# Order of transfers in the first chunk of a fused attention and gated-MLP kernel: weight sets, queries and keys, packed outputs

## The chip, the core and the metric

The kernel runs on one core of a Trainium2 chip. The metric is the device time of one execution in microseconds (us); where several runs stand, it is their median. The engines are TensorE (PE in the profile, with PEld for its weight loads), VectorE (DVE), ScalarE (ACT), GpSimd (POOL) and SyncE (SP), which here only issues transfers. ACT issues a few transfers too. Each engine works through its own instructions in order; engines wait for each other through semaphores. The transfers that SP issues go through one hardware queue, and those of ACT through another.

## The reference

```
x   = A_x                                  # [1, 2048, 576] bf16
xn  = (x - mean) / sqrt(var + 1e-5)        # layer norm over 576, no gain or bias
qkv = xn @ wqkv                            # 32 heads of 18
p   = softmax(mask(q k^T / sqrt(18)))      # causal, and at most 255 positions back
A   = (p v) @ wo
B   = (silu(xn @ w1) * (xn @ w3)) @ w2     # hidden size 4608
out = x + A + B
```

## The kernel before

The 2048 positions are worked in four chunks of 512 (`c` = 0 to 3). A chunk has three stages. First come the projections of q, k and v. Then come 36 units (`u` = 0 to 35), each of which makes 128 of the 4608 hidden columns: nine pairs of matmuls (`n` = 0 to 8 in `unit_pairs`) with 64 rows each, a tanh on ACT (`unit_tanh`) and two operations on DVE (`unit_h`). Last comes a stage that multiplies the hidden values with `w2` and the attention outputs with `wo`, and writes the rows out (`p2_item`).

A pair of a unit multiplies both halves of the partitions at once. Pairs 0 to 3 and 8 read the transposed, normalized input `xnT`; pairs 4 to 7 read `xnS`, a copy of it with the two halves of the partitions swapped, made by two transfers (`xn_swap`).

The attention is woven into the units. The 32 heads stand in 8 groups `g` of four. A score step (`score_step`) is some small matmuls of keys against queries (`scores`, L587), an exponential on ACT (L596) and a mask on POOL (L623); in the first chunk a group has four of them. A planner in the Python code (`spaced_step`, `clock`, `nxt`) decides in which unit and before which pair the next step stands. After the steps of two groups the product with the values follows (`pv`, L644), and its outputs are transposed and scaled on DVE and POOL (`pv_out`, `o_scale`, `o_turn`). `o_pack` and `o_rest` then move them by small transfers (L670) into `oT`, which the last stage reads. Work that a unit owes to a later one is put into a list by `later(u, ...)` and emitted right after `unit_h` of that unit.

Queries and keys come out of the projection into `stage`, and transfers spread them into `qv` and `kv`: `span_main(a, b)` has two transfers of q and three of k for groups a to b-1 (L528), and `span_last(a, b)` one small one for each group (two for group 3), at L557 or L559. A group's first score step needs all of them.

The weights `w1` and `w3` come in sets of 512 hidden columns, four units each. A set is six parts of 192 KB (`load_part`, L322). There are three buffers for sets, and in the first chunk the fourth set goes into a part of `hT`, so set 4 (units 16 to 19) is the first that has to wait for a buffer. `load_w13` emits parts at once; `owed` counts parts to be emitted one by one behind certain pairs of a unit (`owe_part`), each of which may not be issued before the pair's matmul. Rows of the next chunk are loaded by `load_x` (L298) at units given in `loads`; `ln_stats` (L357 to L360) reads them at units given in `plan`: the first of them right after `unit_h` of unit 13 in the first chunk.

The order of SP's queue in the first chunk is therefore written out by hand. It is: four parts of set 1, keys of groups 0 and 1, q of groups 2 to 7, set 2, keys of groups 2 to 7 (three transfers), the first half of set 3, the small transfer of group 2, the second half of set 3, two parts of set 4, the small ones of groups 3 and 4, two parts of set 4, the small ones of groups 5 to 7, two loads of x rows, and the last two parts of set 4. The last two parts of set 1 go through ACT.

Of the kernel before, what the change touches and what calls it, by code (L numbers as in the profile page):

```python
# [164 lines left out]
def bass_parallel_sum__sliding_block__glu_gated_swiglu__prompt_kernel(  # L165
# [20 lines left out]
    G = H // 4  # L186
# [11 lines left out]
    with ExitStack() as es:  # L198
# [17 lines left out]
        xnS = sb("xnS", [128, 4, CH])  # L216
# [3 lines left out]
        w13 = [sb(f"w13_{i}", [128, 9, 512]) for i in range(NW13)]  # L220
# [106 lines left out]
        def load_w13(behind=(), parts=6, eng="sp"):  # L327
            for _ in range(parts):
                load_part((), behind, eng)
# [100 lines left out]
        def xk(c):  # L430
            return [("xnT", c % 2, tt) for tt in range(TB)]
# [100 lines left out]
        def span_main(a, b, q_eng="sp", only=slice(None)):  # L532

            gs_ = list(range(a, b))
            moves = []
            for pr in range(2):
                moves.append(("q", q_eng, gs_, qv[64 * pr:64 * pr + 2 * Dh, a:b, :], stage[2 * Dh * pr:2 * Dh * (pr + 1), a:b, :]))
            for i in range(3):
                r0 = 4 * Dh + i * Dh
                moves.append(("k", "sp", gs_, keys_of(a, b, 64 * (i // 2) + Dh * (i % 2), Dh, i % 2),  # L540
                              stage[r0:r0 + Dh, a:b, :].rearrange("q g (b f) -> q (g b) f", f=KB)))
            span_issue(a, b, moves, True, only)
# [120 lines left out]
        def o_turn(g, half):  # L663
            i = g // 2 % NOD
            c0 = half * (CH // 2)
            add("dve", lambda e: e.transpose(od[i][:, g % 2, c0:c0 + CH // 2], oq[:, c0:c0 + CH // 2]),  # L666
                r=["oq", "oq0"], **{"j" if half or g % 2 else "w": [("od", i)]})
# [36 lines left out]
        def unit_pairs(c, u, n0, n1, b0):  # L704

            fc, fl = divmod(u, 4)
            sl, wt = w13_at(c * NFC + fc)
            for n in range(n0, n1):
                for r in range(2):
                    r0 = 64 * r  # L710
                    k = 8 if n == 8 else (2 * n + r if n < 4 else 2 * (n - 4) + 1 - r)
                    src = xnT[r0:r0 + 64, c % 2, k // 2, :] if n in (0, 1, 2, 3, 8) else xnS[r0:r0 + 64, n - 4, :]
                    op = add("pe", lambda e, n=n, r0=r0, r=r, k=k, src=src: e.matmul(  # L713
                        PS[:, b0 + r, :], wt[r0:r0 + 64, k, fl * 128:(fl + 1) * 128], src,
                        start=(n == 0), stop=(n == 8), tile_position=(r0, 0)),
                        r=[("w13", sl), "xnS"] + xk(c), **{"j" if n else "w": [("ps", b0 + r)]})
            return op

        def unit_tanh(u, b0):
# [93 lines left out]
        for n in range(2):  # L813
            add("sp", lambda e, n=n: e.dma_start(
                wv[:, 2 * n:2 * n + 2, :], A_wqkv[256 * n:256 * n + 256, 2 * D:3 * D].rearrange("(kd p) f -> p kd f", p=128)),
                w=[f"wv{n}"], dma=f"wv{n}")
# [53 lines left out]
        def turn(i):  # L870
# [6 lines left out]
            r=[("sm", 2), "eps"], w=[("sm", 3)])  # L877
# [23 lines left out]
        for h in range(2):  # L901
# [13 lines left out]
            for k0, k1, need, key, which in parts:  # L915
                for n, (dst, src) in enumerate(moves[m] for m in which):
                    dealt.append(add("pool", lambda e, dst=dst[:, k0:k1], src=src[:, k0:k1]: e.tensor_copy(dst, src),
                                     r=need + ([] if dealt else [("xnd", 1)]), **{"j" if n else "w": [key]}))
# [21 lines left out]
        for what in [("q", 0), ("q", 1), ("q", 2), ("q", 3), ("8", 7), None]:  # L940
            got = proj_begin(0, what) if what else proj_end()
            if got == ("v", 3):
                add("pool", lambda e: e.memset(qv[:, 2:G, :].bitcast(dt.float32), 0.0), r=["wp1", "mk"], w=[("q", g) for g in range(2, G)])
                clear_keys(2, G)
                add("pool", lambda e: e.memset(kb4[:, :, :, :].bitcast(dt.float32), 0.0), w=[("kp", g) for g in range(G)])
            elif got == ("q", 0):
                load_w13((), 4)
                span_main(0, 2, "act")
            elif got == ("q", 2):
                load_w13((), 2, "act")  # L950
                span_last(0, 2)

        add("act", lambda e: e.activation(th[0][:, 0:1], neghalf[:], ACT.Tanh), r=["neghalf"], w=[("th", 0)])
        span_main(2, G, "sp", slice(0, 2))

        PV_COST, PV_AFTER = 6.6, 20
        FIRST = {0: 14, 1: 11, 2: 8, 3: 11}
# [3 lines left out]
        for c in range(NC):  # L961
# [5 lines left out]
            stat, apply, xt = ({v[k]: i for i, v in plan.items()} for k in range(3))  # L967
            loads = {8: (2,), 17: (3,)} if c + 1 < NC else {}
            if c == 0:
                loads[6] = (0, 1)  # L970
            total = 9 * NF + len(att) + 3 * PV_COST
            if c:
                total += 9 * sum(COST[kind] for kind, _ in PROJ)
# [2 lines left out]
            nxt = soon = start  # L976
# [14 lines left out]
            def later(u, what):  # L991
                side.setdefault(u, []).append(what)
# [53 lines left out]
            for u in range(NF):  # L1046
# [7 lines left out]
                for n in range(9):  # L1054
                    into = nxt - (clock + 9 - n)
                    if (u, n) == JOINT[c]:
                        ja = 1
                        assert next_pv == ja and ja + 1 in pv_ready and clock + 6 >= pv_ready[ja + 1], (c, next_pv, clock, pv_ready)
                        two = [job(), job()]
                        job_ctr += 1  # L1060
                        kept = []
                        _DEBUG.setdefault("joint", []).append((c, u, n, done, round(clock - pv_ready[ja + 1], 1), len([o for o in P.ops if o.eng == "pe"])))
                        for m, j in enumerate((ja, ja + 1)):
                            pv(c, j, two[m])
                            clock += PV_COST
                            release(j, kept)
                        next_pv = ja + 2
                        if c in (1, 2):
                            nxt = soon = max(nxt, clock + 9)
                        for m, sl in enumerate(kept):  # L1070
                            uqs[2 + m:] = [pt_slot(sl).rearrange("p q r -> p (q r)").bitcast(dt.float32)]
                            uq_keys[2 + m:] = [pt_keys(sl)]
                        pv_out(two[0][0], 0)
                        pv_out(two[0][1], 1)
                        o_scale(0)
                        pv_out(two[1][0], 2)
                        pv_out(two[1][1], 3)
                        g = 2 * ja
                        later(u, lambda g=g: (o_turn(g, 0), o_turn(g, 1), o_scale(1)))
                        later(u + 1, lambda g=g: o_turn(g + 1, 0))  # L1080
                        later(u + 2, lambda g=g, ja=ja: (o_turn(g + 1, 1), o_pack(ja, "sp"), o_scale(2)))
                        later(u + 3, lambda g=g: (o_turn(g + 2, 0), o_turn(g + 2, 1), o_scale(3)))
                        later(u + 3, lambda kept=kept: free.extend(kept))
                        later(u + 4, lambda g=g: o_turn(g + 3, 0))
                        later(u + 5, lambda g=g, ja=ja: (o_turn(g + 3, 1), o_pack(ja + 1, "sp")))
                    if (c == 0 or u or n > 1) and 9 * u + n not in calm and done < len(att) and (free or done < len(early) or done in held) and (clock >= nxt or (n == 8 and into < 3 and clock >= soon)):
                        spaced_step()
                    op = unit_pairs(c, u, n, n + 1, b0[0])
                    clock += 1
                    if (n in (3, 8) or (n == 6 and c == 0 and u < 4)) and (c, u) not in ((1, 26), (2, 24)):  # L1090
                        owe_part(op)
# [3 lines left out]
                if u == FIRST[c]:  # L1095
                    j = next_pv
                    assert j == 0 and clock >= pv_ready[0], (c, clock, pv_ready)
                    next_pv += 1
                    banks = job()
                    pv(c, j, banks)  # L1100
                    clock += PV_COST
                    release(j, None)
                    later(u, lambda b=banks: (pv_out(b[0], 0), pv_out(b[1], 1), o_scale(0)))
                    later(u + 1, lambda j=j: (o_turn(2 * j, 0), o_turn(2 * j, 1), o_scale(1)))
                    later(u + 2, lambda j=j: o_turn(2 * j + 1, 0))
                    later(u + 3, lambda j=j: (o_turn(2 * j + 1, 1), o_pack(j, "sp")))
                    if j == 0:
                        for n in range(7):
                            later(u + 4 + (n if c == 0 else n // 2 + n // 6), lambda n=n: o_rest(n, "sp" if c else "act"))
                unit_h(u, b0[0])  # L1110
                for what in side.pop(u, []):
                    what()
# [6 lines left out]
                if u in apply:  # L1119
                    t = (c + 1) * TB + apply[u]  # L1120
                    ln_apply(t, xslot[t])
                if c == 0 and u == 1:
                    span_main(2, G, "act", slice(2, None))
                if c == 0 and u == 2:
                    span_last(2, G, slice(0, 1))
                if c == 0 and u in (4, 5):
                    span_last(2, G, slice(1, 3) if u == 4 else slice(3, None))
                if c == 0 and u == 13:
                    for t in range(4):
                        a0 = (4 + 14 * (t // 2)) * Dh  # L1130
# [80 lines left out]
```

## Time and profile before

| what | us |
|---|---|
| median of 3 runs | 557.74 |
| lowest and highest | 557.55, 560.05 |
| the profiled execution, device time | 558.27 |
| its span, first to last instruction | 556.5 |
| PE busy in the span | 552.4 (99%) |
| DVE, ACT, POOL busy | 311.1, 259.9, 162.7 |

The difference of 1.8 us between the device time and the span lies outside of what the profile shows as instructions. A row of the timeline gives the start, how long the merged instructions took, the engine (SPq and ACTq are the transfers that SP and ACT issue, and the time is that of issuing), the line, the operation, the tiles written and read, and a count. A row can merge several instructions of one kind. A matmul's end is modelled in the profile, so PE looks busy where it only waits a little: two matmul rows have to be compared by their starts. The weight buffers appear as `w`, and the set that lies in `hT` as `hT`.

### The profile page before, as it was taken

To read this page: it belongs to the slowest core of one execution; us is meant where nothing else is said; L and a number is where in the kernel's file an instruction comes from. 1 tells how busy PE (TensorE), PEld (TensorE's weight loads), DVE (VectorE), ACT (ScalarE), POOL (GpSimd) and SP (SyncE) were. 2 spreads that over 40 slices of the span, in tenths; PEclk is the share of its full clock that TensorE was granted. 3 is DMA by queue.
4 is the path that set the end of the run, shared out by engine and by line. 5 is a ranking of instruction groups with operands and counts; after the bars stand their busy time and mean duration, and the time that the engine had idled before them with its cause. 6 is when DMAs were issued, how large, how long until landed. Compare 5 with 4: busy or idle time off the path is not lost.

```text
span 556.5 us, 15754 instructions
## 1 busy us (share of the span) xinstructions
PE 552.4 (99%) x6772; PEld 349.6 (63%) x6772; DVE 311.1 (56%) x583; ACT 259.9 (47%) x359; POOL 162.7 (29%) x385
## 2 busy tenths in 40 slices
PE   8999999999999999999999999999999999999998
PEld 4676554677654545677766544747776554455776
DVE  6466979610366888851046687874105577678211
ACT  6457766100287774700038787550005777756000
POOL 6423534300034452530003454333000334333000
PEclk9999999999999999999999999999999999999999
DMA  9986999777367459676726639677572673633652
GB/s 246 200 166 166 218 179 197 153 203 182 94 140 154 126 123 182 174 176 177 199 61 139 160 110 174 144 188 177 154 187 54 138 174 107 165 108 103 164 150 65
DMA packets 127216, 85.96 MB, mean 154 GB/s; under 512 B 34451, under 2 KB 124907, under 8 KB 127147
## 3 DMA queue, kind: packets, MB, share of 16 engines
q1 hardware_dynamic: 125107, 83.09, 64.9%
q10 hardware_dynamic: 2040, 1.87, 1.4%
q8 instruction: 53, 0.87, 0.7%
q14 instruction: 16, 0.13, 0.1%
HBM read 71.29 MB, written 2.36 MB: 132 GB/s over the span
## 4 chain that ended last, share of the span: by engine, by line
PE 99%; ACT 0%; DVE 0%; issue 0%
PE ps L713 50%; PE ps L785 25%; PE ps L461 10%; PE ps L587 6%; PE ps L644 3%; PE ps L792 3%; PE ps L827 1%; PE ps L699 0%; PE ps L406 0%; ACT xnT L413 0%; DVE ofin L803 0%; DVE oq L821 0%
## 5 line engine op out<-in xcount | busy, mean ns | idle before, releaser
L713 PE MATMUL ps<-xnT,w 64*128 64x512 bf16 x1400 | 186.2, 376 | 0.0
L713 PE MATMUL ps<-xnS,w 64*128 64x512 bf16 x1120 | 154.5, 376 | 0.0
L785 PE MATMUL ps<-w,hT 128*128 128x288 bf16 x1156 | 146.7, 286 | 0.0
L728 DVE SCALAR_TENSOR_TENSOR gs<-th,ps 128x512 bf16<-128x512 bf16 x144 | 97.8, 679 | 76.8 <-ACT th L722 75.9
L785 PEld LDWEIGHTS ps<-w,hT 128*128 128x128 bf16 x1156 | 112.5, 98 | 28.9 <-issue 0.2
L713 PEld LDWEIGHTS ps<-xnT,w 64*128 64x128 bf16 x1400 | 74.6, 94 | 58.6 <-issue 0.5
L722 ACT ACTIVATE th<-ps 128x512 bf16<-128x512 f32 x144 | 85.6, 595 | 45.1 <-PE ps L713 42.7
L731 DVE SCALAR_TENSOR_TENSOR hT<-gs,ps 128x512 bf16<-128x512 bf16 x144 | 98.9, 687 | 5.0
L713 PEld LDWEIGHTS ps<-xnS,w 64*128 64x128 bf16 x1120 | 59.7, 94 | 45.4
L596 ACT ACTIVATE pt<-ps 128x1024 bf16<-128x1024 f32 (+1 forms) x70 | 70.7, 1010 | 31.4 <-PE ps L587 31.1
L474 ACT ACTIVATE stage<-ps 128x512 bf16<-128x512 f32 x16 | 9.5, 596 | 142.0 <-PE ps L461 142.0
L623 POOL TENSOR_TENSOR hT<-hT,mk 128x128 int32<-128x128 int32 (+1 forms) x59 | 24.0, 429 | 171.4 <-ACT hT L596 171.2
L803 DVE TENSOR_TENSOR ofin<-ps,xp 128x288 bf16<-128x288 f32 x31 | 13.3, 455 | 108.3 <-PE ps L699 58.1
L623 POOL TENSOR_TENSOR pt<-pt,mk 128x128 int32<-128x128 int32 (+1 forms) x124 | 49.9, 427 | 28.8 <-ACT pt L596 28.8
L587 PE MATMUL ps<-qv,kv 64*128 64x320 bf16 (+4 forms) x528 | 53.3, 260 | 0.0
L587 PEld LDWEIGHTS ps<-qv,kv 64*128 64x128 bf16 x528 | 27.7, 94 | 26.2 <-ACT hT L596 1.5
L461 PE MATMUL ps<-xnT,wp 64*128 64x512 bf16 (+1 forms) x360 | 38.1, 355 | 0.0
L596 ACT ACTIVATE w<-ps 128x1024 bf16<-128x1024 f32 (+1 forms) x32 | 32.3, 1010 | 12.2 <-PE ps L587 12.1
L596 ACT ACTIVATE hT<-ps 128x1024 bf16<-128x1024 f32 (+1 forms) x32 | 32.3, 1009 | 5.3 <-PE ps L587 4.8
L623 POOL TENSOR_TENSOR w<-w,mk 128x128 int32<-128x128 int32 (+1 forms) x56 | 22.9, 429 | 28.7 <-ACT w L596 28.7
L666 DVE STREAM_TRANSPOSE od<-oq 128x256 bf16<-128x256 bf16 x64 | 25.8, 427 | 6.9 <-POOL oq L659 6.9
L461 PEld LDWEIGHTS ps<-xnT,wp 64*128 64x128 bf16 x360 | 18.9, 94 | 14.6 <-ACT stage L474 0.3
(93 smaller groups left out, 384.0 us busy)
## 6 DMA issues: line engine op xcount, KB each, us to landing
w<-in_B_w_dram SPq DMA_DIRECT2D x208, 192.0 KB, 4.1
w<-in_B_w_dram SPq DMA_DIRECT2D x72, 288.0 KB, 3.3
xp<-in_A_x_dram SPq DMA_DIRECT2D x30, 144.0 KB, 3.0
out_dram<-ofin SPq DMA_DIRECT2D x31, 72.0 KB, 1.7
xnS<-xnT SPq DMA_DIRECT2D x8, 256.0 KB, 4.2
oT<-od SPq DMA_DIRECT2D x40, 36.0 KB
pt<-in_A_wqkv_dram SPq DMA_DIRECT2D x4, 288.0 KB, 5.6
hT<-in_B_w_dram SPq DMA_DIRECT2D x6, 192.0 KB, 3.6
```

Of the source, the lines that this page charges most:

```text
L461: op = add("pe", lambda e, out_=out_, st=st, mv=mv, n=n, r0=r0, first=first: e.matmul(out_, st, mv, start=first, stop=(part == 1 and n == ...
L587: add("pe", lambda e, r0=r0, out_=out_, kb=kb, q0=q0, nb=nb: e.matmul(out_, kb4[r0:r0 + 64, g, kb + NV - NB, :] if kb < 0 else kv[r0:r0 + ...
L596: add("act", lambda e: e.activation(pt_slot(sl)[:, 0:w, :], PS[:, SC[0]:SC[1] + 1, 0:w].rearrange("p r q -> p q r"), ACT.Exp, scale=scale) ...
L623: add("pool", lambda e, vb=vb, mm=mm: e.tensor_tensor(vb, vb, mm, ALU.mult), r=(key if n == 0 else []) + ["mk"], **{"w" if n == 0 else "j" ...
L644: add("pe", lambda e, p=p, q=q, pr=pr, sl=sl, g=g, pos=pos, q0=q0, nb=nb, col=col, first=first, n=n: e.matmul(PS[32 * q:32 * q + VW, banks ...
L666: add("dve", lambda e: e.transpose(od[i][:, g % 2, c0:c0 + CH // 2], oq[:, c0:c0 + CH // 2]), r=["oq", "oq0"], **{"j" if half or g % 2 els ...
L713: op = add("pe", lambda e, n=n, r0=r0, r=r, k=k, src=src: e.matmul(PS[:, b0 + r, :], wt[r0:r0 + 64, k, fl * 128:(fl + 1) * 128], src, star ...
L722: add("act", lambda e: e.activation(th[i][:], PS[:, bg, :], ACT.Tanh, scale=0.5), r=[("ps", bg)], w=[("th", i)])
L728: add("dve", lambda e: e.scalar_tensor_tensor(out=gs[i][:], in0=th[i][:], scalar=1.0, in1=PS[:, bg, :], op0=ALU.add, op1=ALU.mult), r=[("t ...
L731: add("dve", lambda e: e.scalar_tensor_tensor(out=hT[:, u, :], in0=gs[i][:], scalar=0.5, in1=PS[:, bu, :], op0=ALU.mult, op1=ALU.mult), r= ...
L785: add("pe", lambda e: e.matmul(bank, hT[:, f, tt * 128:(tt + 1) * 128], w2[sl][:, k, n0:n1], start=first, stop=(c + 1 == NC and half == 1 ...
L792: add("pe", lambda e: e.matmul(bank, oT[:, k, tt * 128:(tt + 1) * 128], wo[:, k, d0 + n0:d0 + n1], start=False, stop=(k == 3 and (half == ...
```

## The change

Five things change, most of them in the first chunk.

- All six parts of set 1 are issued by SP (four before, and two on ACT).
- q and keys of groups 2 to 7 (`span_main(2, G)`) are issued by SP after unit 3, behind the twelve owed parts of sets 2 and 3. The small transfers follow after units 4, 5 and 6 (2, 4 and 5 before).
- Two loads of x rows are put at unit 7 (6 before), so behind all of set 4.
- One score step is kept from standing in unit 22 before pair 7.
- In all chunks `o_pack` stands one unit later than the last transposition it reads, as does what follows it (`o_rest`); and only pairs 4 to 7 wait for `xnS`.

```diff
 def unit_pairs
-  r=[("w13", sl), "xnS"] + xk(c)
+  r=[("w13", sl)] + (["xnS"] if 3 < n < 8 else []) + xk(c)
...
 elif got == ("q", 0):
-    load_w13((), 4)
+    load_w13((), 6)
     span_main(0, 2, "act")
 elif got == ("q", 2):
-    load_w13((), 2, "act")
     span_last(0, 2)
...
-span_main(2, G, "sp", slice(0, 2))
...
 if c == 0:
-    loads[6] = (0, 1)
+    loads[7] = (0, 1)
...
-later(u + 2, lambda g=g, ja=ja: (o_turn(g + 1, 1), o_pack(ja, "sp"), o_scale(2)))
-later(u + 3, lambda g=g: (o_turn(g + 2, 0), o_turn(g + 2, 1), o_scale(3)))
+later(u + 2, lambda g=g: (o_turn(g + 1, 1), o_scale(2)))
+later(u + 3, lambda g=g, ja=ja: (o_pack(ja, "sp"), o_turn(g + 2, 0), o_turn(g + 2, 1), o_scale(3)))
...
-later(u + 5, lambda g=g, ja=ja: (o_turn(g + 3, 1), o_pack(ja + 1, "sp")))
+later(u + 5, lambda g=g: o_turn(g + 3, 1))
+later(u + 6, lambda ja=ja: o_pack(ja + 1, "sp"))
...
-if (c == 0 or u or n > 1) and 9 * u + n not in calm and ...
+if (c == 0 or u or n > 1) and (c, u, n) != (0, 22, 7) and 9 * u + n not in calm and ...
...
-later(u + 3, lambda j=j: (o_turn(2 * j + 1, 1), o_pack(j, "sp")))
+later(u + 3, lambda j=j: o_turn(2 * j + 1, 1))
+later(u + 4, lambda j=j: o_pack(j, "sp"))
 if j == 0:
-    later(u + 4 + ..., lambda n=n: o_rest(n, ...))
+    later(u + 5 + ..., lambda n=n: o_rest(n, ...))
...
-if c == 0 and u == 1:
-    span_main(2, G, "act", slice(2, None))
-if c == 0 and u == 2:
-    span_last(2, G, slice(0, 1))
-if c == 0 and u in (4, 5):
-    span_last(2, G, slice(1, 3) if u == 4 else slice(3, None))
+if c == 0 and u == 3:
+    span_main(2, G)
+if c == 0 and u in (4, 5, 6):
+    span_last(2, G, (slice(0, 1), slice(1, 3), slice(3, None))[u - 4])
```

More of the change, by code (lines that the diff above doesn't have):

```diff
@@ L715, in unit_pairs @@
                         start=(n == 0), stop=(n == 8), tile_position=(r0, 0)),
-                        r=[("w13", sl), "xnS"] + xk(c), **{"j" if n else "w": [("ps", b0 + r)]})
+                        r=[("w13", sl)] + (["xnS"] if 3 < n < 8 else []) + xk(c), **{"j" if n else "w": [("ps", b0 + r)]})
             return op
@@ L1080, in bass_parallel_sum__sliding_block__glu_gated_swiglu__prompt_kernel @@
                         later(u + 1, lambda g=g: o_turn(g + 1, 0))
-                        later(u + 2, lambda g=g, ja=ja: (o_turn(g + 1, 1), o_pack(ja, "sp"), o_scale(2)))
-                        later(u + 3, lambda g=g: (o_turn(g + 2, 0), o_turn(g + 2, 1), o_scale(3)))
+                        later(u + 2, lambda g=g: (o_turn(g + 1, 1), o_scale(2)))
+                        later(u + 3, lambda g=g, ja=ja: (o_pack(ja, "sp"), o_turn(g + 2, 0), o_turn(g + 2, 1), o_scale(3)))
                         later(u + 3, lambda kept=kept: free.extend(kept))
                         later(u + 4, lambda g=g: o_turn(g + 3, 0))
-                        later(u + 5, lambda g=g, ja=ja: (o_turn(g + 3, 1), o_pack(ja + 1, "sp")))
-                    if (c == 0 or u or n > 1) and 9 * u + n not in calm and done < len(att) and (free or done < len(early) or done in held) and (clock >= nxt or (n == 8 and into < 3 and clock >= soon)):
+                        later(u + 5, lambda g=g: o_turn(g + 3, 1))
+                        later(u + 6, lambda ja=ja: o_pack(ja + 1, "sp"))
+                    if (c == 0 or u or n > 1) and (c, u, n) != (0, 22, 7) and 9 * u + n not in calm and done < len(att) and (free or done < len(early) or done in held) and (clock >= nxt or (n == 8 and into < 3 and clock >= soon)):
                         spaced_step()
@@ L1105, in bass_parallel_sum__sliding_block__glu_gated_swiglu__prompt_kernel @@
                     later(u + 2, lambda j=j: o_turn(2 * j + 1, 0))
-                    later(u + 3, lambda j=j: (o_turn(2 * j + 1, 1), o_pack(j, "sp")))
+                    later(u + 3, lambda j=j: o_turn(2 * j + 1, 1))
+                    later(u + 4, lambda j=j: o_pack(j, "sp"))
                     if j == 0:
                         for n in range(7):
-                            later(u + 4 + (n if c == 0 else n // 2 + n // 6), lambda n=n: o_rest(n, "sp" if c else "act"))
+                            later(u + 5 + (n if c == 0 else n // 2 + n // 6), lambda n=n: o_rest(n, "sp" if c else "act"))
                 unit_h(u, b0[0])
```

## The prediction

> **What bounds the kernel now.** I read the page first, then PE's waits, then the starts of PE's matmuls in the first chunk, and at last SP's queue.
>
> ```profile
> span 556.5 us, 15754 instructions
> PE 552.4 (99%) x6772; PEld 349.6 (63%) x6772; DVE 311.1 (56%) x583; ACT 259.9 (47%) x359; POOL 162.7 (29%) x385
> ...
> PE 99%; ACT 0%; DVE 0%; issue 0%
> ...
> PE ps L827 <- DVE oq L821: 1.2, 1, 1.2
> PE ps L461 <- ACT xnT L413: 0.5, 1, 0.5
> ```
>
> PE is busy from end to end, it is 99% of the chain that ends last, and its listed waits come to 1.7 us, all ahead of the units. So whatever the change wins must be in small stalls that modelled ends hide. A pair of 512 columns should start 0.22 us after the one before (55.76 to 55.98 below). I looked for starts further apart than this in the four chunks. Beside the products with the values, two places in the first chunk stand out:
>
> ```profile
> 55.76 0.38 PE L713 MATMUL ps<-xnS,hT 64*128 64x512 bf16 x2
> 55.98 0.38 PE L713 MATMUL ps<-xnT,hT 64*128 64x512 bf16 x2
> 56.34 0.82 PE L713 MATMUL ps<-xnT,w 64*128 64x512 bf16 x6
> ...
> 70.20 1.02 ACT L596 ACTIVATE w<-ps 128x1024 bf16<-128x1024 f32 x1
> 70.50 0.83 PE L713 MATMUL ps<-xnS,w 64*128 64x512 bf16 x6
> 71.28 0.40 PE L587 MATMUL ps<-qv,kv 64*128 64x320 bf16 x6
> ```
>
> At 56.34 unit 16 begins: the weights change from `hT` (set 3) to `w` (set 4). It should have begun at 56.20, so 0.14 is lost. At 71.28 a score step stands in unit 22 behind pair 6; it should have begun at 70.50 + 3 x 0.22 = 71.16 and waited for the exponential that ended at 71.22, so 0.12 is lost. The change can win 0.26 us in all. What it may cost must be read from SP's queue:
>
> ```profile
> 20.72 1.68 SPq L559 DMA_DIRECT2D kv<-stage  x2
> 22.51 1.57 SPq L528 DMA_DIRECT2D qv<-stage  x2
> 24.12 4.62 SPq L322 DMA_DIRECT2D w<-in_B_w_dram  x6
> 28.79 0.85 SPq L528 DMA_DIRECT2D kv<-stage  x1
> 29.68 4.32 SPq L528 DMA_DIRECT2D kv<-stage  x1
> 34.04 2.35 SPq L528 DMA_DIRECT2D kv<-stage  x1
> 36.43 3.12 SPq L322 DMA_DIRECT2D hT<-in_B_w_dram  x3
> 39.59 0.83 SPq L557 DMA_DIRECT2D kv<-stage  x1
> 40.46 1.91 SPq L322 DMA_DIRECT2D hT<-in_B_w_dram  x3
> 42.42 1.26 SPq L322 DMA_DIRECT2D w<-in_B_w_dram  x2
> 43.73 2.55 SPq L557 DMA_DIRECT2D kv<-stage  x3
> 46.33 1.98 SPq L322 DMA_DIRECT2D w<-in_B_w_dram  x2
> 48.35 2.52 SPq L557 DMA_DIRECT2D kv<-stage  x3
> 50.92 0.95 SPq L298 DMA_DIRECT2D xp<-in_A_x_dram  x2
> 51.91 1.36 SPq L322 DMA_DIRECT2D w<-in_B_w_dram  x2
> ...
> 19.52 1.42 ACTq L322 DMA_DIRECT2D w<-in_B_w_dram  x2
> ```
>
> SP is never idle here. A part costs it 0.65 (3 in 1.91), a small key transfer 0.84 (2.52 for 3). Two of the big key transfers hold it for 4.32 and 2.35 where the first took 0.85: 5.0 us in which it can only have been waiting for room behind what is in flight. And the x rows, emitted at unit 6, are not issued before 50.92.
>
> **The change, part by part.**
>
> *Weights ahead.* The last two parts of set 4 are issued at 51.91 to 53.27, and PE goes on at 56.34, 3.1 us behind. In the new order they stand ahead of the last small keys and the x rows, some 3 us earlier in SP's time; the stall goes: -0.14. What is late next at unit 16 is DVE, below. Sets 2 and 3 get nearer to the front, so nothing is lost there. ACT loses two issues (1.42 us), and no wait of PE names ACT at that time: nothing.
>
> *q and keys of groups 2 to 7 later.* The third big key transfer leaves SP at 34.04 + 2.35 = 36.39 now. In the new order 8 more parts stand ahead of it (six of set 3, two from ACT). If SP alone set the pace, it would be free at 36.39 - 5.0 + 8 x 0.65 = 36.6: the lower end. If the transfers in flight set it, all that stood ahead is still ahead, and set 3 in addition. Its 6 x 192 KB at full rate:
>
> ```profile
> 29.00:37.00 8.00, 8.00 (x83) 6.22 (x80) 5.24 (x9) 3.87 (x6) 0.73 (x2) 1.00 0.91 166
> 56.00:62.00 6.00, 6.00 (x66) 3.28 (x64) 5.37 (x13) 5.06 (x7) 3.96 (x9) 1.00 1.01 231
> ```
>
> The last figure of a row is GB/s: 1.18 MB at 231 are 5.1 us, so 41.5 is the upper end. The share before it, 0.91 while SP was held, is not far from the 1.01 of the full stretch: the transfers set the pace, and I take a value near that end, 41.0. Group 2's small transfer then follows two parts instead of three: 36.43 to 39.59 was 3.16, less 0.65, so it starts at 41.0 + 2.5 = 43.5 and ends at 44.3. The first score steps of groups 0 and 2, and DVE behind unit 13:
>
> ```profile
> 34.22 0.45 PE L587 MATMUL ps<-qv,kv 64*128 64x320 bf16 x4
> 47.98 0.41 PE L587 MATMUL ps<-qv,kv 64*128 64x320 bf16 x4
> 52.43 0.69 DVE L731 SCALAR_TENSOR_TENSOR hT<-gs,ps 128x512 bf16<-128x512 bf16 x1
> 53.25 0.46 DVE L357 BATCH_NORM_STATS2 stats<-xp 128x6 f32<-128x288 bf16 x1
> 54.90 0.69 DVE L731 SCALAR_TENSOR_TENSOR hT<-gs,ps 128x512 bf16<-128x512 bf16 x1
> ```
>
> A transfer lands some 2.3 us after its issue starts (the x rows: 50.92 to the DVE row at 53.25, which starts 0.13 behind the end of the operation before it where others follow without a gap, so it waited). Under load I allow 3: group 2 is there at 46.5, and at 47.0 by the upper end, ahead of 47.98. Cost 0; the cover is 1 to 1.5 us now where it was some 5 (39.59 + 0.83 + 2.3 = 42.7). Groups 3 and later come four score steps apart. The keys of groups 0 and 1 move behind two parts: their last issue ends at 22.4 + 1.3 = 23.7, and they are used at 34.22; nothing.
>
> *The x rows.* Between the third big key transfer and the x rows SP now has 10 parts and 7 small transfers: 36.39 to 50.92, 14.5 us. In the new order it is 6 parts and 7 small ones: 14.5 - 4 x 0.65 = 11.9. By 41.0 that puts the x rows at 52.9; by the lower end at 48.5, by the upper at 53.4. Of the 14.5 some 1.2 lie in the first issue behind the big keys (3.12 for three, where 1.91 is usual); if that goes too, 51.7. Between 51.7 and 52.9 I take 52.3: 1.4 later than now. The statistics at 53.25 then start at 54.65. Queued behind them on DVE are `unit_h` of unit 14, whose second operation ends at 55.59 and would end at 57.0. Unit 16 needs its PSUM banks: three pairs of banks go round, and the product with the values behind unit 14 takes one. Unit 16 could begin at 56.20, so DVE has 0.6 us to spare, less 0.1 for the step to PE: a delay of 1.4 costs 0.9. The bounds are 0 (no delay, or one under 0.5) and 2.5 - 0.5 = 2.0. I take +0.9.
>
> *The score step in unit 22.* It moves to pair 8 or later, 0.22 behind, where the exponential has ended: -0.11, between 0 and -0.12.
>
> *`xnS` waited for by pairs 4 to 7 alone.* PE never waited for it (the two rows of waits name others): nothing.
>
> *`o_pack` a unit later.*
>
> ```profile
> SPq L670 <- DVE rden L658: 11.7, 3, 7.8
> 91.59 3.15 SPq L670 DMA_DIRECT2D oT<-od  x4
> 99.34 3.10 SPq L670 DMA_DIRECT2D oT<-od  x4
> 118.80 0.65 PE L792 MATMUL ps<-wo,oT 128*128 128x288 bf16 x4
> ```
>
> SP stands still for these transfers, 7.8 us in the longest case, with weight parts behind them. They will stand still less, and the parts go earlier; but PE has no stall there to give back. The last pack in the first chunk ends at 102.4 and is read at 118.8: two us later costs nothing. In the other chunks the order is alike. 0, with bounds of nothing on either side.
>
> The sum: -0.14 - 0.11 + 0.9 = +0.65. The profiled execution took 558.27, so 558.9; the median stands 0.53 below it, so 558.4 in the terms of the median.
>
> **Rivals.** *The x rows are in time.* SP is held less because set 3's parts are large packets and drain ahead of the keys; the third big key transfer is out by 39.5, the rows before 51.4, and DVE stays within its 0.5. For it: SP's own pace would allow 36.6. Against: the 5 us for which it was held. Then only the gain is left: 557.74 - 0.25 = 557.5.
>
> *DVE or the keys late by much.* The side of slower. The same queue, with the big keys not out before 43.7 because their small packets drain slower behind a whole set. Group 2 then lands at 43.7 + 2.5 + 0.8 + 2.3 = 49.3 or a little later, and PE stops some 1.5 us at 47.98. The x rows go out at 55.6, 4.7 later than now; with PE itself 1.5 late they cost 4.7 - 0.5 - 1.5 = 2.7 more. In all some 4.2 - 0.25: 561.7. The point from which it decides is an end of the big keys at about 43: 1.5 us above my upper end. Against: the share of 0.91 shows room in that stretch.
>
> [...]
>
> *The change does nothing.* Set 4 may be held by something else than its place: 557.7.
>
> **How the numbers follow.** Forecast (a stall of 0.3 to 2 us at unit 16) 0.48; x rows in time 0.33; nothing 0.05; much later 0.08; slow PE 0.02; 0.04 for what I do not see, half of it on each side. 0.5% is 2.8 us, about what a measurement of this kernel can tell from no change. All but the two slow rivals lie inside: same 0.87; slower 0.08 + 0.02 + 0.02 = 0.11 with 0.01 of the forecast's upper edge; faster 0.02. The range goes from the rival in time less its uncertainty of 0.4 (557.1) to the forecast with the upper bound (557.74 - 0.25 + 2.0 = 559.5) and 0.5 of spread: 560.0.
>
> **What would show it.** Right: unit 16 begins not with set 4 but with `hT` of unit 14 on DVE, and the statistics of x begin near 54.6 behind a wait for the x rows; the third big key transfer ends near 41 on SP; no wait of PE near 48; no gap in unit 22. Wrong: x rows issued before 51.4, or group 2's scores late behind a transfer.

## The result and the profile after

The changed kernel takes 559.22 us (median of 22 runs), the kernel before 557.83 (22 runs): a ratio of 1.0034, with an interval of 1.0021 to 1.0046. It is 1.4 us slower, which is clear of noise and below the 0.5% that the prediction called no change. Its runs are also further apart: 557.41 to 564.08, against 557.48 to 560.05.

The page of the profiled execution (559.99 us) differs in the chain: part of it no longer runs through PE.

```profile
span 558.3 us, 15754 instructions
PE 551.5 (99%) x6772; PEld 344.1 (62%) x6772; DVE 310.8 (56%) x583; ACT 260.0 (47%) x359; POOL 163.2 (29%) x385
PE 97%; DMA 1%; DVE 1%; SPq 0%; issue 0%; ACT 0%
```

SP's queue in the timeline, from set 3 to the x rows:

```profile
29.28 3.88 SPq L322 DMA_DIRECT2D hT<-in_B_w_dram  x6
33.20 1.66 SPq L528 DMA_DIRECT2D qv<-stage  x2
34.91 6.40 SPq L528 DMA_DIRECT2D kv<-stage  x3
41.35 2.40 SPq L322 DMA_DIRECT2D w<-in_B_w_dram  x2
43.80 0.83 SPq L557 DMA_DIRECT2D kv<-stage  x1
...
52.56 0.48 SPq L298 DMA_DIRECT2D xp<-in_A_x_dram  x1
```

Set 3 is issued in one piece, the three big key transfers end at 41.31, the small one of group 2 starts at 43.80, and the x rows go out at 52.56 where they went out at 50.92. DVE and PE around unit 16:

```profile
52.24 0.69 DVE L731 SCALAR_TENSOR_TENSOR hT<-gs,ps 128x512 bf16<-128x512 bf16 x1
54.86 0.46 DVE L357 BATCH_NORM_STATS2 stats<-xp 128x6 f32<-128x288 bf16 x1 [1.93 <-DMA xp<-in_A_x_dram]
55.84 0.63 DVE L728 SCALAR_TENSOR_TENSOR gs<-th,ps 128x512 bf16<-128x512 bf16 x1
56.51 0.69 DVE L731 SCALAR_TENSOR_TENSOR hT<-gs,ps 128x512 bf16<-128x512 bf16 x1
...
55.77 0.38 PE L713 MATMUL ps<-xnT,hT 64*128 64x512 bf16 x2
57.34 1.02 PE L713 MATMUL ps<-xnT,w 64*128 64x512 bf16 x7 [1.19 <-DVE hT L731]
```

DVE is idle for 1.93 us until the x rows land. Behind their statistics stand the two operations of unit 14; the second ends at 57.20, and unit 16 begins at 57.34. It could have begun at 55.77 + 0.22 = 55.99: a stop of 1.35 us, and PE's wait names DVE. Unit 22 lost its stall: eight matmuls from 71.50, four pairs, and the score step follows them at 72.36.

```profile
71.50 1.04 PE L713 MATMUL ps<-xnS,w 64*128 64x512 bf16 x8
72.36 0.40 PE L587 MATMUL ps<-qv,kv 64*128 64x320 bf16 x6
...
90.06 0.38 PE L713 MATMUL ps<-xnT,w 64*128 64x512 bf16 x2
90.93 0.82 PE L713 MATMUL ps<-xnT,w 64*128 64x512 bf16 x6 [0.49 <-issue]
```

The last row is another matter: between two pairs of one unit PE waited 0.87 - 0.22 = 0.65 us, and the profile names no engine and no transfer for it. The span grew by 1.8 us. Of this 1.2 came at unit 16 (1.35 less the 0.14 that set 4 cost there before), 0.65 at this place and 0.3 at a like one in the second chunk; unit 22 gave 0.1 back, and PE had reached unit 16 some 0.2 earlier in this execution. The wait at 90.93 stands in no other profile, that of the same kernel below (e5_after_again) included, so it belongs to this execution and not to the change. The one in the second chunk (0.36 at 225.75, a score step) comes again at the same step in e6_keys_later (0.25) and e7_both (0.17), which have the changed order of keys, and is not listed in e5_after_again; the profile before loses some 0.2 at that step without a listed wait. Whether the change has a part in it stays open.

### The profile page after: what moved, and what is told of

It is laid out like the page before. It is cut to its first block, busy times and chain, and to the rows that moved or that the text cites. A ratio compares the mean times of both kernels' runs of the same rounds, so it can differ in the third digit from the quotient of the medians.

```text
span 558.3 us, 15754 instructions
## 1 busy us (share of the span) xinstructions
PE 551.5 (99%) x6772; PEld 344.1 (62%) x6772; DVE 310.8 (56%) x583; ACT 260.0 (47%) x359; POOL 163.2 (29%) x385
## 4 chain that ended last, share of the span: by engine, by line
PE 97%; DMA 1%; DVE 1%; SPq 0%; issue 0%; ACT 0%
PE ps L713 49%; PE ps L785 25%; PE ps L461 9%; PE ps L587 6%; PE ps L644 3%; PE ps L792 3%; DMA xp<-in_A_x_dram 1%; SPq L557 0%; PE ps L699 0%; PE ps L406 0%; DVE stats L357 0%; DVE stats L359 0%; ACT xnT L413 0%; DVE hT L731 0%; DVE gs L728 0%
## 5 line engine op out<-in xcount | busy, mean ns | idle before, releaser
L713 PEld LDWEIGHTS ps<-xnT,w 64*128 64x128 bf16 x1400 | 72.0, 94 | 63.1 <-issue 2.4
L713 PEld LDWEIGHTS ps<-xnS,w 64*128 64x128 bf16 x1120 | 57.5, 94 | 47.4
```

## The experiments

The theory was the one of the prediction: the x rows are issued late, the statistics that read them stand ahead of unit 14's work in DVE's order, and unit 16 waits for DVE. The rivals were the later queries and keys, the later packs, and chance.

**The rows early.** The changed kernel with one line as before:

```diff
-                loads[7] = (0, 1)
+                loads[6] = (0, 1)
```

> The changed kernel with the two loads of x rows back at unit 6, all else as changed. Theory (x rows late, DVE's statistics wait, unit 16 waits for DVE): SP issues the rows near 48.6, the statistics start right behind unit 13, no stall at unit 16, about 557.6 us, as before or 0.2 below. Rival (the later queries, keys or packs cost it): stays near 559.2.

Measured: 557.80 us (11 runs, highest 558.25) against 557.80 before (27 runs of before on the same chip), ratio 1.0000 (0.9991 to 1.0009). DVE in the timeline goes straight from unit 13 to the statistics:

```profile
52.13 0.69 DVE L731 SCALAR_TENSOR_TENSOR hT<-gs,ps 128x512 bf16<-128x512 bf16 x1
52.73 0.45 DVE L357 BATCH_NORM_STATS2 stats<-xp 128x6 f32<-128x288 bf16 x1
```

The later queries, keys and packs are all still in this kernel, and the loss is gone. The changed kernel itself was not timed on this chip; on the one where it was timed again, e7_both below, with this line among its two, stands at 557.67 beside 558.62.

**The statistics later.** The changed kernel, rows as late as there, with one line more:

```diff
             near = {t: tuple(...) for t in range(3)} | {3: (34, 35, 40)}
+            if c == 0:
+                near[0] = (14, 15, 16)
```

> The changed kernel, rows as late as there, but the statistics of the first x rows stand behind unit 14 instead of unit 13 in DVE's order. Theory: the wait for the rows falls behind both operations of unit 14, nothing holds unit 16, about 557.6 us. Rival (unit 16 is held by something else, or late rows cost in another way): about 559.2.

Measured: 557.60 us (11 runs, highest 558.05), ratio 0.9995 (0.9986 to 1.0004). The rows go out at 52.77, later than in the changed kernel, and nothing waits:

```profile
52.77 0.95 SPq L298 DMA_DIRECT2D xp<-in_A_x_dram  x2
...
53.41 0.69 DVE L728 SCALAR_TENSOR_TENSOR gs<-th,ps 128x512 bf16<-128x512 bf16 x1 [0.46 <-ACT th L722]
54.14 0.69 DVE L731 SCALAR_TENSOR_TENSOR hT<-gs,ps 128x512 bf16<-128x512 bf16 x1
...
56.11 0.40 DVE L357 BATCH_NORM_STATS2 stats<-xp 128x6 f32<-128x288 bf16 x1
...
55.81 0.38 PE L713 MATMUL ps<-xnT,hT 64*128 64x512 bf16 x2
56.02 1.03 PE L713 MATMUL ps<-xnT,w 64*128 64x512 bf16 x8
```

Unit 16 begins 0.21 behind the pair before it. So late rows cost nothing by themselves; what costs is that DVE waits for them with unit 14's work behind. The two experiments mend opposite ends of the same wait, and each takes the whole loss away.

**The rows later still.** The changed kernel with the rows at unit 9, behind the third load of rows and two parts of set 5:

```diff
-                loads[7] = (0, 1)
+                loads[9] = (0, 1)
```

> The changed kernel with the rows at unit 9, behind two parts of set 5 and the third load of rows (1.8 us more). Theory: each us of delay is a us of PE: stall near 3.2 at unit 16, about 561 us, and if a longer stall brings the slow clock of TensorE, runs with a granted clock under 1.0 and 2 us more become frequent. Rival: no further loss, 559.2.

Measured: 564.63 us (4 runs, 563.64 to 566.05), ratio 1.0124 (1.0109 to 1.0139). This is more than the theory gave. The statistics wait until 57.98, PE stops from 56.07 to 60.46, and then it is slow:

```profile
54.42 1.33 SPq L298 DMA_DIRECT2D xp<-in_A_x_dram  x1
...
57.98 0.46 DVE L357 BATCH_NORM_STATS2 stats<-xp 128x6 f32<-128x288 bf16 x1 [4.98 <-DMA xp<-in_A_x_dram]
...
55.85 0.38 PE L713 MATMUL ps<-xnT,hT 64*128 64x512 bf16 x2
60.46 1.67 PE L713 MATMUL ps<-xnT,w 64*128 64x512 bf16 x8 [4.23 <-DVE hT L731]
```

The windows of this run give, behind the busy times, the granted clock of each stretch, the share of the DMA engines and GB/s:

```profile
50.00:55.80 5.80, 5.80 (x125) 3.37 (x122) 2.61 (x4) 3.94 (x5) 1.02 (x3) 1.00 0.57 155
60.00:64.00 4.00, 3.54 (x22) 1.74 (x24) 3.96 (x11) 0.97 (x1) 2.64 (x8) 0.59 1.11 246
64.00:70.00 6.00, 6.00 (x64) 3.44 (x62) 4.96 (x11) 4.17 (x7) 2.12 (x5) 0.99 0.97 185
```

After the stop of 4.4 us the clock is 0.59 over four us. Microsecond by microsecond from 60 to 65 the windows give 0.87, 0.50, 0.50, 0.50 and 0.93. What these lack of 1.00 adds up to 1.7 us, 0.003 of the execution; that is my estimate of what the lower clock cost here, and by it a mean of 0.994 would be two such stretches. The 2 us of the expectation were an estimate too. In all four runs the mean granted clock of the execution was below 1 (0.997 or 0.994). The rows were issued 1.9 us later than in the changed kernel, as expected, but came 3.1 us later: from the issue to the statistics it was 3.6 us here, and 2.3 there, with two weight parts right ahead.

**The spread of the changed kernel.** The changed kernel again, unaltered.

> The changed kernel once more, for the spread of its runs. Theory: the stall at unit 16 follows the landing of the x rows, which differs between runs; median near 559.2, some runs above 562 with a granted clock of 0.997 or lower (a stop long enough for the slow clock), none of the kernel before so. Rival (the long runs are a chip's mood): long runs in both kernels alike.

Measured: 558.62 us (12 runs, 557.34 to 562.58), ratio 1.0017 (1.0003 to 1.0031), against 557.78 (35 runs, 557.40 to 558.64). The profiled execution happened to be one without loss:

```profile
34.30 5.79 SPq L528 DMA_DIRECT2D kv<-stage  x3
...
51.19 1.43 SPq L298 DMA_DIRECT2D xp<-in_A_x_dram  x3
...
53.47 0.46 DVE L357 BATCH_NORM_STATS2 stats<-xp 128x6 f32<-128x288 bf16 x1 [0.51 <-DMA xp<-in_A_x_dram]
...
55.82 0.38 PE L713 MATMUL ps<-xnT,hT 64*128 64x512 bf16 x2
56.03 1.03 PE L713 MATMUL ps<-xnT,w 64*128 64x512 bf16 x8
```

The same program issued the rows at 51.19, 1.4 us earlier than in the first profile. DVE still waited 0.51, which its slack covered, and set 4 was there too: no stop. So the loss is a race between SP's queue and DVE, and it came out differently in the two profiles. Of the 34 executions of the changed kernel six had a granted clock of 0.997 or 0.994, and these are the ones at 562.3 to 564.1; of the 85 executions of the kernel before whose clock is on record none had. That these six had a stop like the one of 4.4 us in the experiment above would fit: less the estimated 1.7 us for each slow stretch, they stand 3 to 4 us above 557.4. But none of them was profiled, and there is one run against it: of the 11 of e6_keys_later, where the statistics stand behind unit 14 and cannot hold unit 16, one had a clock of 0.997 at 559.64, and that is only 2.3 above the fastest of that kernel, slow clock included. So a lower clock was recorded there with no more than 2.3 us lost in all, and what lowered it in the six is not shown.

**Between.** The third load of rows ahead of the first two:

```diff
-                loads[7] = (0, 1)
+                loads[8] = (2, 0, 1)
```

> The changed kernel with the third load of x rows ahead of the first two: 0.5 us more for the rows that unit 13's statistics read, between the change (rows near 51.2 to 52.6) and unit 9 (a stop of 4.4 us, clock 0.997 or below in every run). Theory: stop at unit 16 some 0.5 longer, median 0.5 to 1.0 above the change's, some 560, and more of the runs with a granted clock under 1.0 than the 6 of 34 of the change, but not all. Rival (the slow clock has nothing to do with the length of the stop): the share stays.

Measured: 558.99 us (12 runs, 557.44 to 565.55) against 558.17 of before on this chip, ratio 1.0026 (1.0003 to 1.0050). Two of 12 runs had the lower clock. The 560 of the theory did not come: the loss is no larger than the changed kernel's. With so few runs two of 12 beside six of 34 tells nothing between the theory and its rival. Its profile again caught an execution in which SP was early (rows issued at 50.71).

**The rows later and nothing else.** The kernel before with the rows at unit 7:

```diff
-                loads[6] = (0, 1)
+                loads[7] = (0, 1)
```

> The kernel before with nothing but the two loads of x rows moved from unit 6 to unit 7. Theory: rows issued near 52.2 (two parts of 0.65 later), statistics near 54.5, unit 16 some 0.8 late less the 0.14 that set 4 cost there: about 558.5 us. Rival: no difference, 557.8.

Measured: 557.85 us (11 runs, 557.54 to 558.68), ratio 0.9999 (0.9989 to 1.0009). The expectation missed. The rows went out at 50.54 and not at 52.2, and the statistics began at 53.70:

```profile
29.95 5.76 SPq L528 DMA_DIRECT2D kv<-stage  x3
...
50.54 1.54 SPq L298 DMA_DIRECT2D xp<-in_A_x_dram  x3
...
53.70 0.46 DVE L357 BATCH_NORM_STATS2 stats<-xp 128x6 f32<-128x288 bf16 x1 [0.75 <-DMA xp<-in_A_x_dram]
...
55.79 0.38 PE L713 MATMUL ps<-xnT,hT 64*128 64x512 bf16 x2
56.19 1.04 PE L713 MATMUL ps<-xnT,w 64*128 64x512 bf16 x8
```

The profile of the kernel before, from which I reckoned, was itself one with late rows: 50.92 there, but 48.60 in the kernel of the experiment e8_rest_alone below, which has the same order ahead of them. The difference lies in the three big key transfers: they held SP for 7.60 us in that profile, the longest of all twelve (4.46 to 7.60), for 5.76 here and for 5.24 in e8_rest_alone. With the two parts added the rows come to the edge of DVE's slack: unit 14's second operation ends at 56.04, and unit 16 begins at 56.19, 0.18 late. In the median nothing is lost. So the place of the rows alone is not enough; it takes both them and the new order of parts and keys ahead of them.

**The keys later.** To see how near group 2's keys came, with the statistics out of the way:

```diff
-                if c == 0 and u == 3:
+                if c == 0 and u == 4:
                     span_main(2, G)
-                if c == 0 and u in (4, 5, 6):
-                    span_last(2, G, (...)[u - 4])
+                if c == 0 and u in (5, 6, 7):
+                    span_last(2, G, (...)[u - 5])
```

> The changed kernel with the statistics of the first x rows behind unit 14, and queries and keys of groups 2 to 7 behind unit 4 instead of 3, the small transfers behind units 5 to 7. The cover of group 2 was put at 1 to 1.5 us. Theory: its last transfer lands near 49, its score step at 47.8 waits some 1.2, about 558.8 us. Rival (more cover than worked out): no stall there, about 557.6.

Measured: 558.64 us (11 runs, 557.38 to 559.64), ratio 1.0009 (0.9999 to 1.0019). The rows of group 1's last and group 2's first score step, of the changed kernel and then of this one:

```profile
46.12 0.35 PE L587 MATMUL ps<-qv,kv 64*128 64x320 bf16 x4
47.82 0.38 PE L587 MATMUL ps<-qv,kv 64*128 64x320 bf16 x4
```

```profile
45.40 0.83 SPq L557 DMA_DIRECT2D kv<-stage  x1
...
46.60 0.39 PE L587 MATMUL ps<-qv,kv 64*128 64x320 bf16 x4
48.43 0.40 PE L587 MATMUL ps<-qv,kv 64*128 64x320 bf16 x4
```

The step comes 1.83 behind the one before instead of 1.70: 0.13 late, with the key transfer issued at 45.40, 1.6 later than in the changed kernel; and PE itself was 0.5 later there. No wait of PE names the keys there. If they are what made it late, they were there 3.0 us after the issue, and the changed kernel had about 1 us of cover; if not, more. The stall of 1.2 that I expected was not there in the profiled run. The median of 558.64 is 0.9 above before, though, and the profiled run itself took 558.64: against the profile of e5_after_again its PE begins the units 0.45 later (21.55 against 21.10), loses 0.13 here and some 0.3 by the second chunk's score step. Whether other executions stop longer at this step is not shown.

**The rest alone.** The kernel before with the packs a unit later, `xnS` waited for by pairs 4 to 7, and unit 22 without a score step ahead of pair 7; weights, keys and rows in the old order. The edit is the diff of the change without its hunks on `load_w13`, `loads`, `span_main` and `span_last`.

> The kernel before with the rest of the change alone: packs a unit later, swapped input waited for by pairs 4 to 7, no score step in unit 22 ahead of pair 7; the order of weights, keys and rows as before. Theory: 0.1 us less at the most, 557.7. Rival (the packs' place costs or gains in the later chunks): a difference of 0.5 or more.

Measured: 557.68 us (11 runs) against 557.78, ratio 0.9999 (0.9990 to 1.0007). These parts change nothing that can be told.

```profile
48.60 1.50 SPq L298 DMA_DIRECT2D xp<-in_A_x_dram  x2
...
55.76 0.38 PE L713 MATMUL ps<-xnT,hT 64*128 64x512 bf16 x2
55.98 1.03 PE L713 MATMUL ps<-xnT,w 64*128 64x512 bf16 x8
```

Unit 16 begins 0.22 behind the pair before it, though the weights stand in their old order: the 0.14 that set 4 cost in the profile of the kernel before is not there. It too goes with when SP comes to set 4: its last two parts are issued at 50.14 in this profile, and at 51.91 in that of the kernel before.

**Two versions meant to win.** The changed kernel with both mends (rows at unit 6, statistics behind unit 14), and the kernel before with the rest of the change and the statistics behind unit 14; the lines are those shown above.

> The changed kernel with both mends: x rows at unit 6 and their statistics behind unit 14. Theory: nothing is left of either stall of unit 16 nor of the one in unit 22; 557.5 us, 0.3 below the kernel before, and no run above 558.5. Rival: as the one mend alone, 557.6 to 557.8.

> The kernel before with packs, swapped input and unit 22 as changed, its old order of weights, keys and rows, and the statistics of the first rows behind unit 14. Theory: of the stalls only the 0.14 of set 4 is left; about 557.6 us, and the runs closer together than those of the kernel before. Rival: 557.8, no gain.

Measured: e7_both 557.67 us (11 runs) against 557.78, ratio 1.0001 (0.9992 to 1.0009), and e10_rest_stat 557.83 (12 runs) against 558.17, ratio 0.9998 (0.9989 to 1.0007). With 557.60 for the statistics alone, three versions stand 0.1 to 0.3 us under the medians of the kernel before on their chips, and no interval excludes no difference. None shows the loss of the changed kernel. The narrower spread that I expected of the last was not found: 557.36 to 559.74, where before had 557.60 to 559.67; and one run of e7_both was at 559.28.

## Why the prediction was right, point by point

- **What bounds the kernel.** PE, with 0.26 us to win in two small stalls: right. Both stalls are gone in the runs without the new one (unit 16 begins 0.21 behind the pair before it in e5_after_again; unit 22 as shown), and none of the versions gains more than some 0.3 us.
- **q and keys later.** I took 41.0 for the end of the third big key transfer, near the upper end at which the transfers in flight set the pace; it was 41.31. In e5_after_again it was 40.09, and over the seven profiles with this order it lies between 39.44 and 41.76, so that 41.31 is in part luck. That the transfers in flight set the pace was my estimate, from the DMA share of 0.91: the rows show how long SP was held (7.60 us before, 6.40 after), and not by what. The small transfer of group 2 was put at 43.5 and started at 43.80. The cover left for its score step was put at 1 to 1.5 us; e6_keys_later makes it about 1 or more.
- **The x rows.** Put at 52.3, issued at 52.56; statistics put at 54.65, begun at 54.86; unit 16 held by unit 14's second operation on DVE, as said. The term of the sum was too small: 0.9 us for the stop, where the profile has 1.35. DVE was 1.6 later and not 1.4, and PE reached unit 16 some 0.2 earlier, so the slack was smaller by that.
- **Set 4 and unit 22.** -0.14 and -0.11: both came as said against the profile before. The second is the change's: the stall stands in e2_x_late_alone (71.16) and in none of the kernels with that part of the change. The first is not a fixed cost of the old order, as e8_rest_alone shows.
- **`xnS` and `o_pack` at nothing.** Right: e8_rest_alone, 0.9999.
- **The median.** Forecast 558.4, measured 559.22: 0.8 more. The same kernel a second time gave 558.62. The loss in the medians is thus 1.4 and 0.8 where I reckoned 0.65; that the second is so near is in part luck. The step that fell short is the x rows' again: I gave them one landing time, and they have a spread of over a us between the two profiles, around the edge of DVE's slack. Some runs lose nothing and others over 4 us; how much of the long ones is due to the rows is not shown.
- **The chances.** For slower, 0.08, 0.02 and 0.02 with 0.01 make 0.13 and not 0.11, which leaves 0.85 for same.
- **The rivals.** "The x rows are in time" is not the likeliest case but it happens: e5_after_again's profile is one. Slow PE, at 0.02, was put too low and as an all-or-nothing case: no run on record then shows what the 0.02 stands for (the page of the kernel before has a granted clock of 0.9 or more in each of its 40 slices, a mean of 1.000), but six of 34 executions of the changed kernel had 0.997 or 0.994, and e4_x_later shows 0.59 over four us behind a stop of 4.4 us, longer than any that I worked out. It is the only profile with a lower clock. "DVE or the keys late by much" was not seen at the keys.

## What to carry to other kernels

An engine that works in order and is nowhere near its limit (DVE, 56% busy) held the bound engine here (DVE idle for 1.93 us, PE stopped for 1.35), because a wait for a transfer stood ahead of work that frees its buffers; look at what is queued behind a wait before changing what the wait is for. Where a transfer's landing sits within a microsecond of its use, one profile shows one draw (the three key transfers held SP for 4.46 to 7.60 us, and the profile that I reckoned from had the 7.60): reckon with its spread, and prefer to move the use (one line here, late rows and no loss) over hoping for the transfer. And in a queue that issues without a pause, as SP's did, every item ahead delayed the last one (1.26 and 1.36 us for two weight parts at 44.67 and 48.59, 2.52 for three small key transfers at 49.99, in the first profile of the changed kernel): count the parts that overtake, not only those that move.

## What the runs showed of the hardware

- After a stop of 4.4 us (e4_x_later) the granted clock of PE was 0.59 from 60 to 64, with 0.87, 0.50, 0.50 and 0.50 in its four us and 0.93 in the one after. The first two pairs behind the stop, at 60.46 and 60.68, still stand 0.22 us apart; at 61.46, 61.89 and 62.32 it is 0.43. The stop of 1.35 us in the first profile of the changed kernel left the mean clock at 1.000.
- A loss of 0.003 in the mean granted clock goes with executions some 3 us longer than the others of the same kernel (562.3 to 563.0 beside 559.2), of 0.006 with some 4.5 us; stop and slow clock together if the estimate above holds. One run of e6_keys_later with 0.997 was only 1.0 above its kernel's median (559.64 beside 558.64).
- PE waited 0.65 us between two pairs of one unit (90.06 to 90.93); the profile lists 0.49 of it as "issue" and names no other engine and no transfer. It came in one profile of the changed kernel and not in the other.
- Issuing the same three key transfers held SP for 4.46 to 7.60 us in the twelve profiles (6.40 and 5.79 in the two of the changed kernel, 7.60 before, as 0.85, 4.32 and 2.35 with what lies between them), while the first of them took 0.82 to 0.85.
